# Gather and scatter of the middle slot's last token tile: from 64 rows to all 128

## The chip, the cores and the metric

The kernel runs on one core of a Trainium2 chip. The metric is device time in microseconds (us) of one execution. A profile of one execution of the kernel before, taken on the chip, stands behind every reading. In its lines PE is TensorE (PEld its weight loads), DVE is VectorE, ACT is ScalarE, POOL is GpSimd and SP is SyncE, whose queue issues the plain DMAs; POOL issues the indirect ones. A number after L is a line of the kernel.

## The reference

Eight batches of eight heads of attention over 576 positions (head size 64), where a score below the row's maximum minus `tau` is dropped; then a mixture of eight experts over the 4608 tokens, each of which goes to the one expert with the largest gate value.

```python
scores = scale * np.matmul(q, k.transpose(0, 1, 3, 2))
thresh = np.max(scores, axis=-1, keepdims=True) - tau
scores = np.where(scores >= thresh, scores, -1000000000.0)
...
logits = x @ w_gate + modality_bias[modality_id]
e_idx = np.argmax(logits, axis=1)
...
for e in range(E):
    mask = e_idx == e
    h = np.maximum(x[mask] @ w1[e], 0.0)
    out[mask] = gate_w[mask, None] * (h @ w2[e])
```

With D = 512 columns and F = 1024 hidden units per expert, the output is a matrix of 4608 rows of 512 floats.

## The kernel before

**Attention** runs over 32 pairs of heads (four per batch). Its result `xs`, one row of 512 floats per token, lies in DRAM.

**Routing.** After each batch the tokens are put into a table `tab` in DRAM: each expert has a stretch of its own in it, and a token's entry (its row number and its gate weight) is written to the next free place of its expert. An entry that no token has taken holds the row number 4608, one past the last row, and the weight 0.

**Slots.** The experts' work is cut into slots: a slot is one expert and a stretch of its table entries. Three widths exist, `SIZES = (512, 320, 256)`. Seven slots (two of 256, five of 512) run beside the attention of later batches. The last stage runs behind the attention: two slots of 512, one of 320 (the middle slot) and one of 256, always in this order. Which expert a slot serves is found on the chip: remainders of more than 320 tokens go to the slots of 512, remainders of 257 to 320 to the middle slot, and smaller ones to the slot of 256. Further slots stand behind a run-time condition, for inputs that need them.

**One slot** is the function `slot`. Its tokens are cut into tiles of 128; `TP(t)` is the number of rows of tile t. A width of 512 has four tiles, 256 has two, and the middle slot has three, of 128, 128 and 64 rows. The steps of a slot:

- `rows`: the slot's table entries are loaded as `tb`, one column per tile, always with 128 entries per tile.
- `gather(t)`: an indirect DMA, issued by POOL (L747), fetches the rows of `xs` that column t of `tb` names into `xg`, one row per partition. An index over the bound `nrow - 1` is skipped, without an error, and its partition keeps what it held.
- `xt(t)`: four transposes on PE (L761) bring `xg` into the form [column, token], and ACT and DVE split it into two parts, `xh` and `xl` (L272, L273).
- `l1`: products with `w1` on PE (L805), then the ReLU and again a split, into `hh` and `hl` (L815, L816). Where the width is no multiple of 128, POOL sets the columns of `hh` and `hl` from the width up to the next multiple of 128 to 0 (L814).
- `l2(g, t, z)`: products with `w2` on PE (L832), in two halves of the hidden units, g = 0 and 1. The tokens of tile t are the stationary side, always 128 wide, so a full 128 rows of PSUM are written. After g = 0 ACT writes PSUM times the gate weight to `y0` (L841); after g = 1 DVE adds its share into `y` (L845), and POOL issues the indirect DMA that scatters the rows of `y` to `out` (L847), again skipping indices over the bound.
- The weights come over SP's queue as `raw` and are split into a rounded part and a residual: in the last stage by ACT (L788) and, for the residual, DVE (`w1l`) or POOL (`w2l`), both at L792.

**Buffers.** In the last stage `xg` has four buffers, `y0` four, `y` two; each is used in turn, and a new use waits until the previous user's readers are through.

**Order.** During the attention PE's order is written out by hand. The order on the other engines, and on all engines in the last stage, is laid out when the program is built, by a planner that takes the instructions in the order of the code's due times, models a cost for each and tracks when buffers come free. In the last stage the code asks for the gathers of a slot well ahead of its transposes.

The change touches `gather` (L747) and the last part of `l2` (L835 to L850) and reaches only tiles with fewer than 128 rows: tile 2 of the middle slot.

Of the kernel before, what the change touches and what calls it, by code (L numbers as in the profile page):

```python
# [11 lines left out]
F32 = mybir.dt.float32  # L12
# [3 lines left out]
U32 = mybir.dt.uint32  # L16
# [8 lines left out]
def _inst(x):  # L25
    return x.ins if hasattr(x, "ins") else x
# [3 lines left out]
def tile_attn_moe(  # L30
# [20 lines left out]
    DM = H * D  # L51
    DF = w1.shape[2]
    N = B * S
    P = 128
# [8 lines left out]
    W = 512  # L63
# [23 lines left out]
    xp = ctx.enter_context(tc.tile_pool(name="xp", bufs=1))  # L87
# [103 lines left out]
    xs = dram.tile([N, DM], F32, name="xs")  # L191
# [58 lines left out]
    def tbank(hold=False):  # L250
        i = next(x for x in line if x not in held)
        line.remove(i)
        line.append(i)
        if hold:
            held.add(i)
        return banks[i]

    def let_go(t):
        for i in range(4):
            if banks[i] is t:  # L260
                held.discard(i)
                line.remove(i)
                line.append(i)
# [450 lines left out]
    def slot(where, group, nrow, WT=W, wq=lambda: wp, nbuf=(4, 3, 5), lo_eng=None, xq=None):  # L714
# [3 lines left out]
        box = {}  # L718
# [3 lines left out]
        def TP(t):  # L722

            return min(P, WT - t * P)
# [17 lines left out]
        def gather(t):  # L742
            def f():
                xg = xt_pool().tile([P, DM], F32, name="xg", bufs=nx[1])
                box[("xg", t)] = xg

                nc.gpsimd.indirect_dma_start(  # L747
                    out=xg[0:TP(t)], out_offset=None, in_=xs[0:nrow, :],
                    in_offset=bass.IndirectOffsetOnAxis(ap=box["tb"][0:TP(t), t, 0:1].bitcast(U32), axis=0),
                    bounds_check=nrow - 1, oob_is_err=False)  # L750
            return f

# [68 lines left out]
        def l2(g, t, z):  # L821
            def f():
                if z == 0:
                    box["ps"] = group()
                nt = TP(t)
                ps = box["ps"]
                ts = slice(t * P, (t + 1) * P)
                f_ = g * F2 + z
                hh, hl = box[("h", f_)]
                wh, wl = box[("w", 2, f_)]  # L830
                for y, (h, w) in enumerate(((hh, wh), (hh, wl), (hl, wh))):
                    nc.tensor.matmul(out=ps, lhsT=h[:, ts], rhs=w, start=(z == 0 and y == 0),  # L832
                                     stop=(z == F2 - 1 and y == 2))
                if z < F2 - 1:
                    return  # L835
                let_go(ps)
                ps = ps[0:nt]
                tb = box["tb"][0:nt]
                if g == 0:
                    y0 = xp.tile([P, DM], F32, name="y0", bufs=W // P)[0:nt]  # L840
                    nc.scalar.activation(out=y0, in_=ps, func=AF.Copy, scale=tb[:, t, 1:2].bitcast(F32))  # L841
                    box[("y0", t)] = y0
                    return
                y = xp.tile([P, DM], F32, name="y", bufs=2)[0:nt]
                nc.vector.scalar_tensor_tensor(out=y, in0=ps, scalar=tb[:, t, 1:2].bitcast(F32),  # L845
                                               in1=box.pop(("y0", t)), op0=ALU.mult, op1=ALU.add)
                i = _inst(nc.gpsimd.indirect_dma_start(  # L847
                    out=out, out_offset=bass.IndirectOffsetOnAxis(ap=tb[:, t, 0:1].bitcast(U32), axis=0),
                    in_=y, in_offset=None, bounds_check=N - 1, oob_is_err=False))
                for o in prev_out:  # L850
                    tc.declare_no_dep(i, o, reason="every token has a row of its own")
                prev_out.append(i)
            return f
# [111 lines left out]
    for n0, (w, nb) in zip(begins, SIDE):  # L965
# [12 lines left out]
        def when(u):  # L978

            if u < 0:  # L980
                return n0 + u * C['neg'] * W / w
            k = bisect.bisect_right(times, u) - 1
            nxt = times[k + 1] if k + 1 < len(times) else times[k] + 0.5
            x = k + min(1, (u - times[k]) / (nxt - times[k]))
            kf = math.floor(x)
            a, b = step_of(k0 + kf), step_of(k0 + kf + 1)
            return a + (x - kf) * (b - a) - 0.5
        for e in ev:

            if e[0] is None:  # L990
                t = n0 + e[2]
            elif n0 in begins[:-1]:

                which, f_ = e[3]
                t = n0 + C['w' + 'SL'[w == W]][8 * which + f_ - 8] - e[2]
            else:
                t = when(e[0]) - e[2]
# [49 lines left out]
    with tc.manual_schedule(engines={ET.PE}):  # L1047

        ps = tbank()
# [86 lines left out]
```

## Time and profile before

| | us |
|---|---|
| median of three runs | 1117.74 (1115.88 to 1118.3) |
| the profiled execution | 1116.18 |
| its span, first to last instruction | 1114.5 |

How to read what follows: the page gives each engine's busy time with its share of the span, then the span in 40 equal slices (one digit each, the busy share in tenths; for PEclk the clock granted to TensorE), the DMA queues, and shares of the chain of work that ended last, followed back from the last instruction. Timeline rows are start, duration, engine, line, operation, tile written and tiles read, and in brackets the idle time of that engine before it with what ended it. In rows of groups, "x16 | 12.0, 748 | 19.7" is the count, the busy time in us, the mean ns of one, and the idle time before them in us. Queue q0 is that of the indirect DMAs.

### The profile page before, as it was taken

What the parts mean: (1) busy time and instruction counts of PE and PEld (TensorE: products, weight loads), DVE (VectorE), ACT (ScalarE), POOL (GpSimd) and SP (SyncE); (2) the same over time, 40 slices, a digit from 0 to 9 for tenths busy, and PEclk for the clock granted to TensorE, in tenths of its full rate; (3) what the DMA queues carried; (4) which work ended last, traced back from release to release, by engine and by line L of the source; (5) the groups of instructions that cost most, each with busy time, mean ns of one, the idle gap of its engine ahead of it and who ended that gap; (6) DMA issues with size and microseconds to landing.
All of it is one profiled execution on the core that took longest, in us unless ns stands there. A gap on an engine that the chain in (4) does not pass through costs nothing.

```text
span 1114.5 us, 20778 instructions
## 1 busy us (share of the span) xinstructions
PE 1029.7 (92%) x6683; PEld 809.9 (73%) x6683; DVE 725.7 (65%) x1773; ACT 641.9 (58%) x1474; POOL 537.9 (48%) x727
## 2 busy tenths in 40 slices
PE   7799869989798989999999999999999997999993
PEld 6676647777676767787777777777767775788883
DVE  6788857787568756876676766776677645243441
ACT  5687657666565656666666666566656523434440
POOL 2232345464655563665355644565265546442440
PEclk8999989999899999999999999999999999999997
DMA  5656557656666757476635763676465214644330
GB/s 123 140 136 160 124 128 184 165 110 165 165 161 130 180 129 184 102 202 162 168 82 141 197 161 91 148 206 147 107 141 152 97 39 134 216 145 131 131 99 21
DMA packets 212646, 156.06 MB, mean 140 GB/s; under 512 B 100782, under 2 KB 172462, under 8 KB 212528
## 3 DMA queue, kind: packets, MB, share of 16 engines
q1 hardware_dynamic: 205392, 135.72, 49.1%
q0 software_dynamic: 7136, 18.92, 5.2%
q8 instruction: 55, 0.90, 0.3%
q14 instruction: 63, 0.52, 0.1%
HBM read 84.12 MB, written 19.35 MB: 93 GB/s over the span
## 4 chain that ended last, share of the span: by engine, by line
PE 57%; DVE 3%; issue 2%; DMA 2%; ACT 1%; POOL 1%; another core or an unknown queue 0%; POOLq 0%; ACTq 0%; SPq 0%
PE bk L458 8%; PE bk L832 8%; PE bk L805 8%; PE s L369 8%; PE pm L832 7%; PE pm L805 6%; PE bk L420 6%; PE bk L761 1%; PE bk L311 1%; DVE pr L404 1%; PE bk L449 1%; DVE nm L386 1%; ACT e L392 1%; DMA xg<-xs,tb 1%; PE bk L507 1%
## 5 line engine op out<-in xcount | busy, mean ns | idle before, releaser
L386 DVE TENSOR_REDUCE nm<-s 128x1 f32<-128x576 f32 x288 | 216.9, 754 | 135.1 <-PE s L369 125.2
L392 ACT ACTIVATE e<-s,nm 128x576 f32<-128x576 f32 x288 | 215.0, 747 | 113.8 <-DVE nm L386 107.2
L404 DVE SCALAR_TENSOR_TENSOR pr<-s,nm,e 128x576 f32<-128x576 f32 x288 | 231.5, 815 | 75.1 <-ACT e L392 67.4
L369 PE MATMUL s<-km,q 128*128 128x288 f32 x1024 | 202.3, 320 | 41.1 <-DMA q<-nq 17.2
L431 ACT COPY ptm<-bk 128x512 f32<-128x512 f32 x256 | 149.3, 584 | 78.4 <-PE bk L420 66.4
L369 PEld LDWEIGHTS s<-km,q 128*128 128x128 f32 x1024 | 148.5, 192 | 62.1 <-issue 33.5
L420 PE MATMUL bk<-ident,pr 128*128 128x128 f32 x1152 | 175.8, 276 | 3.9 <-ACT ptm L431 2.0
L420 PEld LDWEIGHTS bk<-ident,pr 128*128 128x128 f32 x1152 | 143.6, 142 | 27.9 <-DVE hl L816 3.0
L458 PE MATMUL bk<-ptm,v_m 128*64 128x320 f32 (+1 forms) x1024 | 144.5, 420 | 0.1
L792 POOL TENSOR_TENSOR w2l<-raw,w2h 128x512 fp32r<-128x512 f32 x88 | 113.7, 1299 | 30.9 <-ACT w2h L788 26.7
L458 PEld LDWEIGHTS bk<-ptm,v_m 128*64 128x64 f32 x1024 | 67.6, 139 | 50.1 <-issue 10.3
L790 POOL CAST w2h<-raw 128x512 fp32r<-128x512 f32 x56 | 34.2, 613 | 140.1 <-DMA raw<-in_moe_w_dram 71.1
L433 ACT COPY rp<-pr 128x64 f32<-128x64 f32 x256 | 59.3, 248 | 56.5 <-DVE pr L404 47.0
L805 PE MATMUL bk<-xh,w1h 128*128 128x512 f32 (+1 forms) x212 | 85.5, 403 | 1.1 <-ACT xh L272 0.9
L805 PE MATMUL bk<-xl,w1h 128*128 128x512 f32 (+1 forms) x212 | 77.3, 365 | 1.9 <-DVE xl L273 1.9
L805 PE MATMUL bk<-xh,w1l 128*128 128x512 f32 (+1 forms) x212 | 76.9, 363 | 0.0
L747 POOL DMA_INDIRECT xg<-xs,tb x37 | 38.2, 1034 | 79.3 <-DMA tb<-tab 55.6
L832 PE MATMUL bk<-w2h,hh 128*128 128x512 f32 x176 | 75.7, 430 | 0.0
L847 POOL DMA_INDIRECT out_dram<-y,tb x37 | 38.6, 1042 | 74.4 <-DVE y L845 53.2
L792 POOL TENSOR_TENSOR w1l<-raw,w1h 128x512 fp32r<-128x512 f32 x56 | 71.8, 1285 | 2.9
L832 PE MATMUL bk<-w2h,hl 128*128 128x512 f32 x176 | 69.4, 394 | 0.0
L792 DVE TENSOR_TENSOR w1l<-raw,w1h 128x512 fp32r<-128x512 f32 x32 | 29.0, 908 | 61.5 <-ACT w1h L788 52.0
(205 smaller groups left out, 2006.7 us busy)
## 6 DMA issues: line engine op xcount, KB each, us to landing
raw<-in_moe_w_dram SPq DMA_DIRECT2D x176, 256.0 KB
q<-nq SPq DMA_DIRECT2D x124, 256.0 KB
km<-nk SPq DMA_DIRECT2D x124, 144.0 KB
v_m<-in_v_dram SPq DMA_DIRECT2D x32, 256.0 KB
xs<-xr SPq DMA_DIRECT2D x32, 256.0 KB
k_m<-in_k_dram SPq DMA_DIRECT2D x62, 128.0 KB
q_m<-in_q_dram SPq DMA_DIRECT2D x62, 128.0 KB
vr<-in_v_dram SPq DMA_DIRECT2D x64, 16.0 KB
```

The lines of the kernel that those rows point to most:

```text
L369: nc.tensor.matmul(out=sps[:, hf, 0:SH], lhsT=a, rhs=x, start=(z == 0), stop=(z == len(passes) - 1))
L386: in_line(nc.vector.tensor_reduce(out=nm[:, 0:1], in_=sv, axis=AX.XY, op=ALU.max, negate=True), two)
L392: nc.scalar.activation(out=e, in_=sv, func=AF.Exp, bias=nm[:, 0:1])
L404: in_line(nc.vector.scalar_tensor_tensor(out=pr.rearrange("p (a x) -> p a x", a=2), in0=s2[n % 2][:, :, 0:SH], scalar=nm[:, 1:2], in1=e, o ...
L420: nc.tensor.transpose(out=ps[:, kc * P:(kc + 1) * P], in_=pr[:, kc * P:(kc + 1) * P], identity=ident)
L431: nc.scalar.copy(out=ptm[:, s, :, (c % 2) * P:(c % 2 + 1) * P], in_=pv)
L433: nc.scalar.copy(out=rp[:, i, :], in_=pr[:, SA:S])
L458: nc.tensor.matmul(out=o, lhsT=lhsT, rhs=rhs, start=start, stop=stop, skip_group_check=True)
L792: eng.tensor_tensor(out=lo, in0=raw, in1=hi.bitcast(F32), op=ALU.subtract)
L805: nc.tensor.matmul(out=ps[:, 0:WT], lhsT=a[:, cs], rhs=x[:, c, :], start=(c == 0 and z == 0), stop=(c == KC - 1 and z == 2))
L832: nc.tensor.matmul(out=ps, lhsT=h[:, ts], rhs=w, start=(z == 0 and y == 0), stop=(z == F2 - 1 and y == 2))
L847: i = _inst(nc.gpsimd.indirect_dma_start(out=out, out_offset=bass.IndirectOffsetOnAxis(ap=tb[:, t, 0:1].bitcast(U32), axis=0), in_=y, in_o ...
```

## The change

The gather of a tile fills all 128 partitions of `xg` with all 128 entries of `tb`'s column, where it took the first `TP(t)`; `y0`, `y` and the weights `tb` are no longer cut to `TP(t)` rows, so that ACT, DVE and the scatter work on 128 partitions. Table entries past the slot's width hold the row number 4608, which lies over both bounds. The transposes of `xt` still read `TP(t)` rows.

```diff
                 nc.gpsimd.indirect_dma_start(
-                    out=xg[0:TP(t)], out_offset=None, in_=xs[0:nrow, :],
-                    in_offset=bass.IndirectOffsetOnAxis(ap=box["tb"][0:TP(t), t, 0:1].bitcast(U32), axis=0),
+                    out=xg, out_offset=None, in_=xs[0:nrow, :],
+                    in_offset=bass.IndirectOffsetOnAxis(ap=box["tb"][:, t, 0:1].bitcast(U32), axis=0),
                     bounds_check=nrow - 1, oob_is_err=False)
...
-                nt = TP(t)
                 ps = box["ps"]
...
                 let_go(ps)
-                ps = ps[0:nt]
-                tb = box["tb"][0:nt]
+                tb = box["tb"]
                 if g == 0:
-                    y0 = xp.tile([P, DM], F32, name="y0", bufs=W // P)[0:nt]
+                    y0 = xp.tile([P, DM], F32, name="y0", bufs=W // P)
                     nc.scalar.activation(out=y0, in_=ps, func=AF.Copy, scale=tb[:, t, 1:2].bitcast(F32))
...
-                y = xp.tile([P, DM], F32, name="y", bufs=2)[0:nt]
+                y = xp.tile([P, DM], F32, name="y", bufs=2)
                 nc.vector.scalar_tensor_tensor(out=y, in0=ps, scalar=tb[:, t, 1:2].bitcast(F32),
                                                in1=box.pop(("y0", t)), op0=ALU.mult, op1=ALU.add)
```

## The prediction

> **What bounds the kernel now.** I read the page first: its span, the busy row, the tenths of PE and of its clock, the chain that ended last.
>
> ```profile
> span 1114.5 us, 20778 instructions
> PE 1029.7 (92%) x6683; PEld 809.9 (73%) x6683; DVE 725.7 (65%) x1773; ACT 641.9 (58%) x1474; POOL 537.9 (48%) x727
> PE   7799869989798989999999999999999997999993
> PEclk8999989999899999999999999999999999999997
> q0 software_dynamic: 7136, 18.92, 5.2%
> PE 57%; DVE 3%; issue 2%; DMA 2%; ACT 1%; POOL 1%; another core or an unknown queue 0%; POOLq 0%; ACTq 0%; SPq 0%
> ```
>
> TensorE is busy 92% of the span and carries 57% of the chain; POOL, which issues the two DMAs that change, is busy 48% and carries 1%. But these are averages, and the change touches a single place: one of 37 gathers and one of 37 scatters. So I went to that place. The order of the 13 gathers in POOL's timeline of the last stage (four for each 512-row slot, three for the middle slot, two for the last) makes the eleventh the gather that changes; of the scatters it is the third from the end. These are the rows around both, with the first gather of the stage for comparison; columns are start, duration, what ran, and the idle time before it with what ended it.
>
> ```profile
> 932.27 1.06 POOL L747 DMA_INDIRECT xg<-xs,tb  x1 [5.53 <-DMA tb<-tab]
> ...
> 993.00 1.01 POOL L747 DMA_INDIRECT xg<-xs,tb  x1 [0.31 <-issue]
> 994.34 0.96 POOL L747 DMA_INDIRECT xg<-xs,tb  x1 [0.33 <-PE bk L761]
> 995.61 1.04 POOL L847 DMA_INDIRECT out_dram<-y,tb  x1 [0.30 <-DVE xl L273]
> 996.67 3.80 POOL L792 TENSOR_TENSOR w2l<-raw,w2h 128x512 fp32r<-128x512 f32 x3
> ...
> 1003.16 1.03 POOL L847 DMA_INDIRECT out_dram<-y,tb  x1 [0.17 <-issue]
> 1017.93 5.04 POOL L792 TENSOR_TENSOR w2l<-raw,w2h 128x512 fp32r<-128x512 f32 x4 [13.73 <-ACT w2h L788]
> 1034.00 1.01 POOL L847 DMA_INDIRECT out_dram<-y,tb  x1 [11.04 <-DVE y L845]
> 1036.80 0.99 POOL L847 DMA_INDIRECT out_dram<-y,tb  x1 [1.79 <-DVE y L845]
> 1038.09 1.05 POOL L747 DMA_INDIRECT xg<-xs,tb  x1 [0.30 <-issue]
> ...
> 1074.58 5.55 POOL L792 TENSOR_TENSOR w2l<-raw,w2h 128x512 fp32r<-128x512 f32 x4 [0.19 <-ACT w2h L788]
> 1080.29 1.19 POOL L847 DMA_INDIRECT out_dram<-y,tb  x1 [0.16 <-issue]
> 1095.32 1.00 POOL L847 DMA_INDIRECT out_dram<-y,tb  x1 [13.83 <-DVE y L845]
> ```
>
> So the gather runs at 994.34 and the scatter at 1080.29. What limits that stretch is in the busy time by windows: before the gather, and from it to the last product.
>
> ```profile
> core 0: us, PE busy (x) PEld busy (x) DVE busy (x) ACT busy (x) POOL busy (x), PEclk, DMA share, GB/s
> 900.00:994.34 94.34, 86.12 (x392) 66.43 (x391) 41.61 (x98) 32.06 (x57) 47.59 (x46) 0.98 0.45 136
> 994.34:1097.09 102.75, 102.71 (x536) 87.32 (x534) 40.40 (x60) 42.98 (x79) 41.40 (x49) 1.00 0.36 114
> ```
>
> From 994.34 to 1097.09 PE is busy 102.71 of 102.75 us at full clock: 0.04 us idle in all, with DVE, ACT and POOL below half. The change removes no matmul, so there is nothing to win there but those 0.04 us, and a loss needs something that stalls PE. Pieces of the chain in order of time (start, duration, work), and PE's two rows that matter below (both are transposes of a gathered tile, L761), complete the picture.
>
> ```profile
> 1030.14 6.30 PE pm L832 x27
> ...
> 1091.46 5.61 PE pm L832 x24
> 1097.09 0.76 DVE y L845
> 1097.88 0.50 POOLq L1029
> 1098.39 0.71 POOL out_dram L847
> ```
>
> ```profile
> 939.25 0.63 PE L761 MATMUL bk<-ident,xg 128*128 128x128 f32 x4 [2.55 <-DMA xg<-xs,tb]
> ...
> 1039.81 0.46 PE L761 MATMUL bk<-ident,xg 64*128 64x64 f32 x4
> ```
>
> After the last product come the y of the last slot's second tile and its scatter. The profiled execution took 1116.18 us, 1.68 more than its span and 1.56 under the median of the three runs (1117.74); a change of the span is added to either.
>
> **The change part by part.** By instructions nothing is added or removed: one gather, one scatter, one ACT and one DVE operation each go from 64 to 128 partitions. The transposes stay at 64 rows, and the last product always filled 128 rows of PSUM.
>
> Which rows are real? Routing the reference's inputs (default seed) by hand gives 1820, 2289 and 499 tokens to three experts; after the side slots 284, 753 and 499 are left. The middle slot takes the 284: its third tile has 28 real rows. Of its 64 rows 36 are skipped by index already; the change adds 64 rows, and these are empty with any inputs, since this slot is only given to remainders of at most 320.
>
> Does a skipped row cost anything? Queue q0 moved 18.92 MB (the middle number of its row); gathers and scatters of 4608 rows of 2 KB are 2 x 4608 x 2048 = 18.87 MB, and the table's 4608 rows of 8 bytes are 0.04. The 64 rows that before already skips in each direction (13 and 15 in the last tiles of the slots with 499 and 241 tokens, 36 here) would be another 0.26: they are not moved. On POOL the gather with 36 skipped of 64 took 0.96 us and the one with 15 of 128 (1038.09) took 1.05.
>
> ```profile
> L747 POOL DMA_INDIRECT xg<-xs,tb x37: 958/1032/1263, 144.2 to 1038.1; - x37
> L747 POOL DMA_INDIRECT xg<-xs,tb x34: 996/1031/1263, 144.2 to 993.0; - x34
> L847 POOL DMA_INDIRECT out_dram<-y,tb x37: 982/1027/1298, 268.8 to 1098.1; - x37
> L841 ACT ACTIVATE y<-pm,tb 128x512 f32<-128x512 f32 x12 | 8.3, 688 | 16.7 <-PE pm L832 16.7
> L841 ACT ACTIVATE y<-pm,tb 64x512 f32<-64x512 f32 x1 | 0.7, 685 | 0.1
> L845 DVE SCALAR_TENSOR_TENSOR y<-pm,tb,y 128x512 f32<-128x512 f32 x16 | 12.0, 748 | 19.7 <-PE pm L832 16.0 <-issue 3.6
> L845 DVE SCALAR_TENSOR_TENSOR y<-pm,tb,y 64x512 f32<-64x512 f32 x1 | 0.7, 743 | 0.0
> ```
>
> These are minimum, median and maximum ns of each kind of issue (the second row: the gathers before ours alone), then the groups of L841 and L845 by shape.
>
> *Gather on POOL.* It is the shortest of its 37 (958 ns). A 128-row list costs 996 to 1263, so +0.04 to +0.30 us; I take the median, +0.07. Below nothing is excluded, as no list of 128 is shorter. Queued behind it are a scatter, four residuals of w2 and a gather, then POOL idles 13.73 us. Those residuals are for the products that start at 1030.14, 27 us after POOL is through with them at 1003.16. Cover for the +0.07: 13.7 us.
>
> *Gather's landing.* The trace has no landing time for it. Upper bound: the first gather of the stage, started at 932.27, let PE go at 939.25, so 6.98 us from start to use, PE's order included. Ours starts at 994.34 and is used at 1039.81: 45.47 us, a margin of 38.5. Even doubled, the landing stays hidden. Cost between 0 and 7 us late, 0 on the path.
>
> *ACT and DVE.* +3 ns (688 for 685) and +5 ns (748 for 743): partitions cost no time. Both engines are under half busy in this window and PE waits for neither. If the cover were gone, 8 ns.
>
> *Scatter.* Now 1.19 us, and 128-row ones take 0.98 to 1.30: -0.21 to +0.11, taken as +0.07 like the gather. After it POOL idles 13.83 us. Its landing matters only to the y of the last slot's second tile, at 1097.09, which reuses its buffer (two buffers in turn): 1097.09 - (1080.29 + 1.19) = 15.6 us of cover, and this y is on the final chain. That is the closest point of the change to the end.
>
> *Waits.* None is new: each buffer was handed over as a whole tile before, and its previous user was a full tile; the gather's own release at 994.34 is already PE's transpose of such a one.
>
> [...]
>
> *Sum:* 0.07 + 0.07 on POOL and 0.008 on ACT and DVE, all beside PE; on the path 0.0. Profiled execution 1116.2, median **1117.7 us**.
>
> **Rivals.**
>
> *Slower: the planner moves the gather.* Outside PE's hand-written part, the order on each queue is laid out when the program is built, with a modelled cost for each instruction; a list twice as long may weigh more. Place: PE's transposes at 1039.81. The point: POOL must start the gather before 1039.81 - 6.98 = 1032.8. Behind the residuals at 1017.93 it still would; behind the two scatters at 1034.00 and 1036.80, where the last slot's gather stands now (1038.09), it would be used at 1045.07, and PE stands 5.3 us: 1117.7 + 5.3 = **1123.0**. For: PE did stand 2.55 us for such a gather at 939.25. Against: the code asks for this gather early, and 38 us is far for a small change of weight.
>
> *Faster: a planner's shift the other way.* Between 900 and 994 PE idles 8.2 us, 2.55 of it before a gathered tile. If the new weights reordered that stretch so that this wait went, 1117.7 - 2.55 = **1115.2**. Against: everything there is issued ahead of the changed gather.
>
> *The change doesn't do what it says:* the 64 rows are fetched and written after all, 2 x 0.13 MB. At the 114 GB/s of the window that is 1.1 us each, under covers of 38 and 15 us: **1117.7** again, and seen only in q0's bytes (19.18 MB).
>
> *A skipped row costs as much as a moved one.* Then the scatter is at worst twice its 1.30 us, and a landing that fits the 7.0 us bound of the gather doubles: 1080.29 + 2.6 + 14 = 1096.9, still ahead of 1097.09: **1117.7**.
>
> **How the numbers follow.** Forecast (all covered) 0.85, rows moved or charged after all 0.04 (same time), planner slower 0.07, planner faster 0.04. What a measurement of this kernel can tell from no change is about 0.2%, 2.2 us; the three runs before spread over 1115.88 to 1118.3, 2.4 us, so a pair of medians without any difference falls outside on either side some 3 or 4 times in 100. That gives faster 0.04 + 0.04 = 0.08, slower 0.07 + 0.04 = 0.11, within 0.81. The unknown costs add nothing to the range, since their covers are larger than their upper ends; it is the runs' spread around 1117.7, widened to touch the faster rival and half of the way to the slower one: 1115.3 to 1120.2. The 1123.0 is left out.
>
> **What would show it.** Right: PE idle under 0.1 us between the gather and the last product; that gather near 1.03 us and that scatter between 0.98 and 1.30, both in the same places of POOL's order; q0 still 18.92 MB; y at 128x512 near 748 ns. Wrong: a wait of PE at L761 for xg in the middle slot; a wait of the last y for the scatter; PE's 8.2 idle us before 994 gone or grown, which would mean that the order was laid out anew.

## The result, and the profile after

| | before | after |
|---|---|---|
| median, us | 1117.24 (4 runs, 1115.88 to 1118.3) | 1108.01 (4 runs, 1106.0 to 1109.11) |
| the profiled execution, us | 1116.18 | 1106.0 |
| its span, us | 1114.5 | 1104.3 |

The ratio of the times is 0.9916, with a 95% interval of 0.9895 to 0.9937: the changed kernel is 0.84% faster. The forecast was no change, 1117.7 us, in a range from 1115.3 to 1120.2; the measured time lies 7.3 us under its lower end. One run of before among those taken beside the experiments was slow, 1444.78 us at a granted clock of 0.653 where the others have 0.970 to 0.979, and is left out of every median and ratio.

The page of the changed kernel, the lines that answer to those shown of before:

```profile
span 1104.3 us, 20778 instructions
PE 1030.8 (93%) x6683; PEld 810.8 (73%) x6683; DVE 724.6 (66%) x1773; ACT 641.5 (58%) x1474; POOL 536.7 (49%) x727
PE   7799869989799899999999999999999997999997
PEclk8999989999999999999999999999999999999999
q0 software_dynamic: 7200, 18.92, 5.2%
```

The instructions are as many as before, and each engine is busy for the same time within 1.2 us. A span that is 10.2 us shorter with equal work means that waiting went, and the row of PE says where: its last digit was 3 and is 7. The last slice of the span, some 28 us, held mostly idle time of PE before, and holds less now. Queue q0 moves the same 18.92 MB in 64 packets more.

Busy time by windows in the changed kernel: from the changed gather to the last product, and from there to the end of the span.

```profile
core 0: us, PE busy (x) PEld busy (x) DVE busy (x) ACT busy (x) POOL busy (x), PEclk, DMA share, GB/s
993.34:1096.06 102.72, 102.69 (x536) 87.33 (x534) 40.38 (x60) 42.97 (x79) 41.42 (x49) 1.00 0.37 113
1096.06:1104.30 8.24, 0.00 (x0) 0.00 (x0) 0.75 (x1) 0.00 (x0) 0.99 (x1) 0.81 0.15 54
```

The same view of before, its second window alone (the first stands in the prediction):

```profile
1097.09:1114.50 17.41, 0.00 (x0) 0.00 (x0) 0.75 (x1) 0.00 (x0) 0.98 (x1) 0.63 0.07 26
```

The stretch that the prediction worked on takes 102.72 us where it took 102.75. The one behind it takes 8.24 us where it took 17.41, with the same two instructions in it, one y on DVE and one scatter on POOL: 9.17 us, as much as the medians differ (1117.24 - 1108.01 = 9.23). The remaining 1.03 us of the spans' difference had come about before the last product. The time up to the last product wanders from execution to execution (it ends between 1095.4 and 1101.5 us in the twelve profiles of this document), so this 1 us isn't put down to the change.

What fills a stretch in which no engine computes? Not the busy rows but POOL's queue rows show it: instructions that the page doesn't count as busy. Each row has the line (a helper's), the operation, its count, the minimum, median and maximum in ns, and the first and last start in us. Before:

```profile
L1102 POOLq INC_SWDGE_SEM  x1: 2468/2468/2468, 1101.7 to 1101.7; - x1
L1132 POOLq DRAIN  x3: 40/107/9375, 1104.2 to 1114.2; - x3
```

And after:

```profile
L1100 POOLq INC_SWDGE_SEM  x1: 348/348/348, 1102.3 to 1102.3; - x1
L1130 POOLq DRAIN  x3: 40/107/718, 1102.7 to 1104.0; - x3
```

Before, a semaphore increment runs from 1101.7 to 1104.2, and then the longest of three drains, which comes first of them, from 1104.2 to 1113.6, 0.9 us before the end of the span. (The expectations below call it the last drain.) After, these two take 0.35 and 0.72 us: 2.12 + 8.66 = 10.78 us less. Something is given back ahead of them. POOL's timeline of the changed kernel:

```profile
992.00 1.01 POOL L747 DMA_INDIRECT xg<-xs,tb  x1 [0.31 <-issue]
993.34 1.00 POOL L747 DMA_INDIRECT xg<-xs,tb  x1 [0.33 <-PE bk L761]
994.64 1.03 POOL L845 DMA_INDIRECT out_dram<-y,tb  x1 [0.30 <-DVE xl L273]
...
1079.25 1.26 POOL L845 DMA_INDIRECT out_dram<-y,tb  x1 [0.15 <-issue]
1094.29 0.98 POOL L845 DMA_INDIRECT out_dram<-y,tb  x1 [13.78 <-DVE y L843]
1098.56 0.99 POOL L845 DMA_INDIRECT out_dram<-y,tb  x1 [3.29 <-issue]
```

And the last row of the same view of before:

```profile
1098.12 0.98 POOL L847 DMA_INDIRECT out_dram<-y,tb  x1 [1.80 <-DVE y L845]
```

Before, the last scatter started 0.28 us after its y (1097.09 + 0.75 = 1097.84). After, y ends at 1096.81 and the scatter starts at 1098.56, 1.75 us later, and the idle time is no longer put down to y but to "issue": POOL waited for nothing that the profile shows. The chain of the changed kernel, in order of time, says the same: its end passes no y and no product any more, but the scatter before it and POOL's own time.

```profile
1094.29 0.98 POOL out_dram L845
1095.27 3.08 issue
1098.36 0.50 POOLq L1027
1098.86 0.69 POOL out_dram L845
```

So 10.78 us were won and 1.75 - 0.28 = 1.47 lost, 9.31 in all; the windows say 9.17. Where the time went is thereby clear, and why the same instructions became shorter is not: nothing in the diff names them.

### The profile page after: what moved, and what is told of

It reads as the page before. It is cut to its first block, busy times and chain, and to the rows that moved or that the text cites. A ratio compares the mean times of both kernels' runs of the same rounds, so it can differ in the third digit from the quotient of the medians.

```text
span 1104.3 us, 20778 instructions
## 1 busy us (share of the span) xinstructions
PE 1030.8 (93%) x6683; PEld 810.8 (73%) x6683; DVE 724.6 (66%) x1773; ACT 641.5 (58%) x1474; POOL 536.7 (49%) x727
## 3 DMA queue, kind: packets, MB, share of 16 engines
q0 software_dynamic: 7200, 18.92, 5.2%
## 4 chain that ended last, share of the span: by engine, by line
PE 73%; DVE 10%; issue 6%; DMA 4%; POOL 4%; ACT 2%; SPq 0%; another core or an unknown queue 0%; POOLq 0%; DVEq 0%; ACTq 0%
PE s L369 13%; PE bk L458 12%; PE bk L805 10%; PE bk L831 9%; PE bk L420 9%; PE pm L831 6%; PE pm L805 5%; DVE pr L404 3%; DVE nm L386 2%; PE bk L311 2%; DMA xg<-xs,tb 2%; PE bk L761 1%; PE bk L449 1%; ACT e L392 1%; DMA q<-nq 1%
## 5 line engine op out<-in xcount | busy, mean ns | idle before, releaser
L845 POOL DMA_INDIRECT out_dram<-y,tb x37 | 38.3, 1035 | 72.9 <-DVE y L843 52.5
L831 PE MATMUL bk<-w2l,hh 128*128 128x512 f32 x176 | 69.5, 395 | 0.0
## 6 DMA issues: line engine op xcount, KB each, us to landing
km<-nk SPq DMA_DIRECT2D x124, 144.0 KB
```

Source lines behind the costliest of these rows:

```text
L845: i = _inst(nc.gpsimd.indirect_dma_start(out=out, out_offset=bass.IndirectOffsetOnAxis(ap=tb[:, t, 0:1].bitcast(U32), axis=0), in_=y, in_o ...
```

## The experiments

**The theory** (theory A of the expectations) is a supposition: POOL keeps a record of every indirect DMA that it has issued, in a room that is limited. When the room runs out, it clears what is finished; if it never does, the records stay until the end, and the increment and the long drain go through all of them. No row of a profile shows such records or their room: they are what the theory adds, and the runs test what follows from them. The kernel issues 114 indirect DMAs (40 into the table, 37 gathers, 37 scatters). Before, with 112 lists of 128 rows and two of 64, would just fit and never run out; after, with 114 of 128, would run out at the last scatter. The gain would be an accident of the last bytes of the room, and either half of the change alone could do nothing. With less room before should end as after does, and with more room after as before does.

What a list takes is an estimate from where the room ran out in the runs below, if the room is as large as the program asks and every list of 128 rows takes the same. With 16128 bytes it ran out at the 112th DMA (e5, by the wait ahead of it), so a list takes at least 16128 / 112 = 144.0 bytes; with 10240 at the 72nd (e6, by the drain: (4148 - 882) / 82 = 39.8, so 40 more than the 3 of e5), so it takes less than 10240 / 71 = 144.2. The 100th DMA with 14336 bytes (e9, by the wait ahead of it) agrees. Two lists of 64 rows with 112 of 128 ran out of 16256 bytes at the last DMA (e3), so one of 64 takes 51 to 136 bytes. Where the program asks for no size, after runs out at its 114th list, so the room is more than 113 lists and at most 114, between 16272 and 16442 bytes. The expectations count in places, nine to a list of 128 rows, which are the 144 bytes here; no run shows a place by itself.

**The rivals.** One of the two halves does it by itself: the gather of full lists, or y, `y0` and scatter on 128 partitions. Or any other change of code or layout would shift the end of the program as well.

The edits of the room's size all change one argument of the program; the number is in bytes:

```diff
-    nc = _bacc.Bacc("TRN2", target_bir_lowering=False, num_devices=1)
+    nc = _bacc.Bacc("TRN2", target_bir_lowering=False, num_devices=1, dynamic_dma_scratch_size=16256)
```

All runs in one table; POOL's queue rows, from which increment and drain are read, follow below. "Tail" is the time from the last product to the end of the span in the profiled execution, a ratio is to runs of before taken beside that run on the same chip (their medians were 1117.49 for e1 to e4, 1116.86 for e5, e6, e8 and after again, and 1117.16 us for e9 and e10), and a dash stands where there was one run alone. Where the room ran out is inferred from the waits and the drains.

| run | room asked for, bytes | ran out at DMA | increment, ns | drain, ns | tail, us | median, us | ratio, 95% |
|---|---|---|---|---|---|---|---|
| before | none | never | 2468 | 9375 | 17.4 | 1117.24 | |
| after | none | 114 | 348 | 718 | 8.2 | 1108.01 | 0.9916 (0.9895 to 0.9937) |
| e1 gather only | none | never | 2468 | 9375 | 17.6 | 1118.39 | 0.9996 (0.9973 to 1.002) |
| e2 scatter only | none | never | 2468 | 9375 | 17.4 | 1117.04 | 0.9994 (0.9969 to 1.0019) |
| e3 before, less room | 16256 | 114 | 348 | 718 | 8.1 | 1106.3 | 0.9897 (0.9854 to 0.994) |
| e4 after, more room | 16640 | never | 2468 | 9375 | 17.3 | 1117.7 | 0.9994 (0.9968 to 1.0019) |
| after again | none | 114 | 348 | 718 | 8.4 | 1106.17 | 0.9909 (0.9883 to 0.9936) |
| e5 after, 16128 | 16128 | 112 | 388 | 882 | 7.0 | 1104.85 | 0.9893 (0.9869 to 0.9916) |
| e8 before, one more | none | 115 of 115 | 348 | 718 | 8.3 | 1108.97 | 0.9922 (0.9897 to 0.9948) |
| e6 before, 10240 | 10240 | 72 | 1188 | 4148 | 10.9 | 1108.06 | – |
| e9 after, 14336 | 14336 | 100 | 628 | 1862 | 8.0 | 1106.42 | – |
| e10 after, 4096 | 4096 | 113, the last time | 368 | 800 | 6.9 | 1108.1 | 0.9911 (0.988 to 0.9943) |

### One half of the change at a time

The first has only the first part of the diff, the gather of all 128 entries:

```diff
-                    out=xg[0:TP(t)], out_offset=None, in_=xs[0:nrow, :],
-                    in_offset=bass.IndirectOffsetOnAxis(ap=box["tb"][0:TP(t), t, 0:1].bitcast(U32), axis=0),
+                    out=xg, out_offset=None, in_=xs[0:nrow, :],
+                    in_offset=bass.IndirectOffsetOnAxis(ap=box["tb"][:, t, 0:1].bitcast(U32), axis=0),
```

> The change's gather alone: tile 2 of the middle slot is gathered with 128 indices, its y and scatter stay at 64 rows. [...] Theory B (a list of 64 rows leaves something behind that the drain pays for): one of two is gone, so the drain is about halved, and the time is near 1112 us; or all of the gain is here, near 1108.

POOL's queue rows of this kernel:

```profile
L1102 POOLq INC_SWDGE_SEM  x1: 2468/2468/2468, 1101.2 to 1101.2; - x1
L1132 POOLq DRAIN  x3: 40/107/9375, 1103.7 to 1113.7; - x3
```

The second has only the rest of the diff, `y0`, `y`, the weights and the scatter on 128 partitions:

```diff
-                ps = ps[0:nt]
-                tb = box["tb"][0:nt]
+                tb = box["tb"]
```

> The change's y and scatter alone on 128 partitions; the gather stays at 64 indices. [...] Theory B: about 1112 us, or 1108 if the scatter's list was all of it.

Its queue rows:

```profile
L1100 POOLq INC_SWDGE_SEM  x1: 2468/2468/2468, 1101.8 to 1101.8; - x1
L1130 POOLq DRAIN  x3: 40/107/9375, 1104.3 to 1114.2; - x3
```

Both have before's increment and drain to the ns, and neither differs from before in time. So neither half does it by itself: the 0.84% needs both, which rules out the first rival. Halves without an effect whose sum has one speak for a threshold.

### The threshold moved to either side

Before, with the room cut to 16256 bytes (the diff above). No instruction of the kernel changes.

> [...] Theory B and theory C (the instructions lie otherwise in memory and are fetched at another time): 1117 us, as no list and no instruction differs.

POOL's queue rows of this kernel:

```profile
L1102 POOLq INC_SWDGE_SEM  x1: 348/348/348, 1102.4 to 1102.4; - x1
L1132 POOLq DRAIN  x3: 40/107/718, 1102.8 to 1104.1; - x3
```

The changed kernel, with 16640 bytes:

> The changed kernel, but with 16640 bytes per partition for the descriptors: 1040 places. Theory A: its 1026 places fit, nothing is cleared, POOL's last drain takes about 9.4 us again and the time is near 1117 us, so that the whole gain is gone. Theories B and C: 1108 us, as after the change.

Its queue rows:

```profile
L1100 POOLq INC_SWDGE_SEM  x1: 2468/2468/2468, 1102.0 to 1102.0; - x1
L1130 POOLq DRAIN  x3: 40/107/9375, 1104.5 to 1114.5; - x3
```

The two have changed places: the code of before, with less room, has the end of the changed kernel and is 1% faster; the code of the change, with more room, has the end of before and is no faster. The last scatter went along. In POOL's timeline of before with less room it has 3.28 us of idle time put down to "issue" in front of it:

```profile
1098.77 0.99 POOL L847 DMA_INDIRECT out_dram<-y,tb  x1 [3.28 <-issue]
```

and in that of the changed kernel with more room it follows its y again:

```profile
1098.48 0.98 POOL L845 DMA_INDIRECT out_dram<-y,tb  x1 [1.82 <-DVE y L843]
```

The partitions, the lists and the skipped rows have no part in the gain beyond the room that they take. The second rival falls too: no instruction and no list was changed in either of the two.

### One DMA more

If the room decides, a DMA that does nothing useful must make before faster. This one gathers 128 rows of 256 bytes early in the attention into a tile that nothing reads, one more list of 128:

```diff
+    more_ix = iota([P, 1], [[0, 1]], "more_ix", cm=1, dt=I32)
+    more_to = glob.tile([P, D], F32, name="more_to")
+
+    def one_more():
+        nc.gpsimd.indirect_dma_start(
+            out=more_to, out_offset=None, in_=q.rearrange("b h s d -> (b h s) d"),
+            in_offset=bass.IndirectOffsetOnAxis(ap=more_ix.bitcast(U32), axis=0),
+            bounds_check=N - 1, oob_is_err=False)
...
+    at(40, one_more)
```

> The kernel before with one more indirect DMA, a gather of 128 rows of 256 bytes of q into a tile that nothing reads, early in the attention. [...] Theory A: the last drain falls to 0.7 us and the kernel gets 9 to 10 us faster by doing more work, near 1108 us. If only the reserved bytes of e3 mattered, and not the count, it stays at 1117 to 1119.

POOL's queue rows of this kernel:

```profile
L1112 POOLq INC_SWDGE_SEM  x1: 348/348/348, 1107.9 to 1107.9; - x1
L1142 POOLq DRAIN  x3: 40/107/718, 1108.3 to 1109.5; - x3
```

With one useless DMA added the kernel is 0.8% faster than before (ratio 0.9922, 0.9897 to 0.9948), and its queue rows are those of the changed kernel. The room was left as it was, so the effect doesn't hang on the bytes that are set aside. The rows stand 5.5 us later than after the change, since in this profiled execution, the slowest of the four, the last product ended that much later (1101.5 for 1096.0); apart from the two instructions that were added, the order of every engine is that of before.

### Where the clearing falls

The changed kernel again, and beside it the same with 16128 bytes, where the room runs out at the 112th DMA, two before the end. That is the scatter at 1079.25 in the timeline above, behind which POOL has some 13 us to spare.

> The changed kernel itself beside the others on the same chip: 0.990 to 0.993 of the kernel before, POOL's last drain 0.7 us.

> The changed kernel with 16128 bytes per partition for the descriptors: 1008 places, so that the room runs out at the 112th of the 114 indirect DMAs (112 x 9 = 1008), the scatter of the middle slot's tile 2, behind which POOL idles 13.8 us, and no longer at the last one. Theory A: the clearing hides there, the last scatter follows its y within 0.3 us instead of 1.75, POOL's last drain finds two or three records more than in the changed kernel (about 0.9 us for 0.7), and the kernel is 1 to 1.5 us faster than the changed one, near 1106.5. If the late start of the last scatter comes from something else (an instruction fetch), it stays, and the time is that of the changed kernel.

The queue rows with 16128 bytes:

```profile
L1100 POOLq INC_SWDGE_SEM  x1: 388/388/388, 1101.0 to 1101.0; - x1
L1130 POOLq DRAIN  x3: 40/107/882, 1101.4 to 1102.9; - x3
```

And POOL's timeline of the same kernel:

```profile
1081.20 0.99 POOL L845 DMA_INDIRECT out_dram<-y,tb  x1 [1.97 <-DVE hl L816]
1094.42 0.98 POOL L845 DMA_INDIRECT out_dram<-y,tb  x1 [12.22 <-DVE y L843]
1097.22 0.98 POOL L845 DMA_INDIRECT out_dram<-y,tb  x1 [1.82 <-DVE y L843]
```

The wait has moved two rows up: 1.97 us ahead of the scatter at 1081.20, where after had 0.15, and the last scatter follows its y as it did before. What the clearing costs, 1.8 us there (the scatter's own row is 0.27 us shorter than in after), is taken from idle time, and the tail is 6.97 us instead of 8.24. The releaser named at 1081.20, `hl`, shows how such a row misleads: a clearing has no name in the profile. The lowest median of all is this one, 1104.85, but the runs of the two (1103.67 to 1106.9, and 1102.97 to 1110.8 for the changed kernel beside it) overlap, so that the 1.3 us between them are shown by the trace and not by the times.

### How the price goes with the records

Before with 10240 bytes, where the room runs out at the 72nd DMA:

> The kernel before with 10240 bytes per partition for the descriptors: 640 places, which run out at the 72nd of 114 indirect DMAs, so that 43 records are left at the end. Theory A, if a clearing takes away all finished records: the last drain is 43/114 of the way up from 0.7 to 9.4 us, about 3.7 to 4 us, and the increment before it between 0.35 and 2.47 us. If a clearing takes only as many as the next DMA needs, the drain stays near 9 us, against the 0.7 of e3.

POOL's queue rows of this kernel:

```profile
L1102 POOLq INC_SWDGE_SEM  x1: 1188/1188/1188, 1100.1 to 1100.1; - x1
L1132 POOLq DRAIN  x3: 40/107/4148, 1101.3 to 1106.1; - x3
```

The drain of 4148 ns lies above the 3.7 to 4 us expected, and the reason is in the sizes, which can now be read. Of the DMAs issued since the room last ran out, the one at which it did included, there are 1 in after, 3 with 16128 bytes and 43 with 10240, and 114 where it never did. The increments lie on one line, 20 ns each, and so do the drains, 81.67 ns each: (4148 - 882) / 40 = 81.65, (882 - 718) / 2 = 82. From 43 to 114 both rise by less than that, as if by 64 records: (9375 - 4148) / 81.67 = 64.0 and (2468 - 1188) / 20 = 64. So a clearing leaves 7 older records, and n is 8, 10, 50 and 114: drain = 65 + 81.67 n, increment = 188 + 20 n. The 7 is worked out from this fit; no row shows the records. Two more rooms, for the changed kernel, tested it: 14336 bytes (out at the 100th, n = 15 + 7 = 22) and 4096 (by the 144 bytes and the 7 out five times, from the 29th on, last at the 113th, n = 2 + 7 = 9).

> The changed kernel with 14336 bytes per partition for the descriptors: 896 places, which run out at the 100th indirect DMA. The four drains so far (9375, 4148, 882 and 718 ns) and the four increments before them (2468, 1188, 388 and 348) all lie on 65 + 81.67 n and 188 + 20 n, if n is the number of DMAs since the clearing, the one that ran out among them, plus 7 older records that a clearing leaves, and 114 where none took place. Here n = 15 + 7 = 22: a drain of 1.86 us and an increment of 0.63. If the drain is set otherwise, by the room left or by time, it needn't lie on that line.

POOL's queue rows with 14336 bytes:

```profile
L1100 POOLq INC_SWDGE_SEM  x1: 628/628/628, 1101.3 to 1101.3; - x1
L1130 POOLq DRAIN  x3: 40/107/1862, 1102.0 to 1104.4; - x3
```

> The changed kernel with 4096 bytes per partition: 256 places, which run out at the 29th indirect DMA and, if a clearing leaves 7 records beside the one that ran out, at every 21st after it: 50, 71, 92 and 113. So n = 8 + 1 = 9 at the end: a drain of 0.80 us and an increment of 0.37, and five clearings of 21 records in place of one of 106. If a clearing's cost goes with the records it clears, each takes some 0.3 us where one took about 1.5, hardly any of it on the path, and the time is that of e5_ring_112, about 1.3 us under the changed kernel. If a clearing has a fixed cost near 1.5 us, the one at the 92nd, a gather of the last stage, and the one at the 113th may show, and the time is at or over the changed kernel's.

And with 4096:

```profile
L1100 POOLq INC_SWDGE_SEM  x1: 368/368/368, 1106.3 to 1106.3; - x1
L1130 POOLq DRAIN  x3: 40/107/800, 1106.7 to 1108.1; - x3
```

The fit gives both to the ns: 188 + 20 x 22 = 628 and 65 + 81.67 x 22 = 1862; 368 and 800 for n = 9. As a time, the second is a miss: its tail is the shortest of all, 6.9 us, yet its median is 1108.1, no better than after. POOL's timeline has, for the 28th and the 29th DMA, both into the table, with 4096 bytes

```profile
465.93 1.00 POOL L617 DMA_INDIRECT tab<-pay,posi  x1 [2.44 <-DVE pk_r L632]
467.23 0.98 POOL L617 DMA_INDIRECT tab<-pay,posi  x1 [0.30 <-issue]
```

and in the changed kernel

```profile
460.11 1.00 POOL L617 DMA_INDIRECT tab<-pay,posi  x1 [2.44 <-DVE pk_r L632]
461.42 0.97 POOL L617 DMA_INDIRECT tab<-pay,posi  x1 [0.30 <-issue]
```

so this profiled execution was 5.8 us behind before the 29th DMA, at which the room first runs out by that estimate. (That DMA into the table, the 28th of before's, starts between 458.7 and 464.2 us in the other eleven profiles.) Four clearings later, at the 112th DMA, it is 5.4 us behind (1084.70 for 1079.25), so in this trace no delay has built up over them. Nor did the first of them cost anything that can be seen: the 29th DMA has 0.30 us of idle time ahead of it in both kernels. The one at the 113th DMA is to be seen, ahead of the last scatter but one:

```profile
1100.21 0.98 POOL L845 DMA_INDIRECT out_dram<-y,tb  x1 [14.25 <-DVE y L843]
```

It starts 0.76 us after its y has ended, where after has 0.28, so this clearing of some 21 records cost 0.48 us. Why the median is no lower than after's stays open; the slower stretch of this execution lies ahead of all clearings, and of the other five runs there is no trace.

The clearing with 14336 bytes is to be seen in the timeline of that kernel, ahead of the gather that had 0.31 us of idle time before it in after (at 992.00 there):

```profile
993.47 1.02 POOL L747 DMA_INDIRECT xg<-xs,tb  x1 [1.14 <-PE pm L831]
```

It cost 0.8 us of POOL's time, while PE was busy.

## Why the prediction was wrong, point by point

**The step that failed is where the sum ends.** The prediction followed the path to the last product, and behind it named "the y of the last slot's second tile and its scatter" as what comes. After that scatter, at 1099.10, the span still had 15.4 us to run, and the chain's last row, which ends there, was quoted without a question to the 15.4. They went into the sum as a constant, part of the span of before ("a change of the span is added to either"), without a reason why they should stay. Of them 11.84 us were the increment and the drain, and these depend on the room taken by the DMAs, two of which the change widens. In place of a term of 0.0 the runs showed -9.2 us behind the last product: -2.12 and -8.66 for the two, +1.47 for the clearing ahead of the last scatter (-9.31 together, 0.14 us beyond what the windows say).

**"By instructions nothing is added or removed"** held, and was the wrong thing to count. A skipped row moves no bytes, but the longer list takes more room: q0 has 64 packets more for the 128 rows that are newly skipped, in the same 18.92 MB. The question "does a skipped row cost anything?" was answered by bytes and by time at issue; the answer that mattered was room, by the estimate 144.0 to 144.2 bytes for each of the two lists where one of 64 rows takes 51 to 136.

**What held.** PE idled 102.72 - 102.69 = 0.03 us between the gather and the last product, for 0.1 forecast as the limit. The gather took 1.00 us (1.03 forecast), the scatter 1.26 (0.98 to 1.30), and the order of every engine is that of before, the widths of the lists aside, so both planner rivals fell; PE's idle time from 900 to the gather, 8.2 us in before, is 93.34 - 85.51 = 7.8. The bytes of q0 stayed, so the rows weren't moved. The groups of L839 and L843 (L841 and L845 before) now have one shape each:

```profile
L839 ACT ACTIVATE y<-pm,tb 128x512 f32<-128x512 f32 x13 | 8.9, 687 | 16.1 <-PE pm L831 15.9
L843 DVE SCALAR_TENSOR_TENSOR y<-pm,tb,y 128x512 f32<-128x512 f32 x17 | 12.7, 748 | 19.7 <-PE pm L831 19.7
```

with the forecast 748 ns for y. Behind the gather a second scatter (1003.16, in the rows shown) stands in POOL's queue, which the prediction's list of what is queued there leaves out; it changes no cover. All of it cost nothing, and e4, the whole change with the end of before, is the clean measurement of that: 0.9994 (0.9968 to 1.0019), the forecast "no change".

**Still open:** why a clearing leaves 7 records, and what sets its price. It was 1.47 us at the 114th DMA of after, 1.8 at the 112th with 16128 bytes and 0.8 at the 100th with 14336, for some 106, 104 and 92 records by the fit; with 4096 bytes it was 0.48 at the 113th and nothing to be seen at the 29th, for some 21 each. So it doesn't go by their number alone. Releasing the records in other ways than by a smaller room was not tried.

## What to carry to other kernels

Follow the span to its end: subtract the end of the last computing instruction from it, and if more than a few us are left (here 15.4 behind the last scatter), look up what the queues of the engines do there, since here busy rows and the chain left these instructions out. In a kernel with many indirect DMAs, find by runs how much room their lists take, and set the room so that it runs out shortly before the end, where POOL is idle: here 16128 bytes gave the shortest median, 1104.85 us, with the changed code (by the times not to be told from the changed kernel itself), and 16256 gave 1106.3 with the code of before, 1.1 and 1.0% under before. A gain that stands at such a threshold belongs to the threshold, not to the edit that crossed it: one DMA more (e8) or a room of 16640 bytes (e4) would have shown another verdict for the same change.

## What of the hardware was not expected

- The end of this program pays for its indirect DMAs: by the fit 81.67 ns in the long drain and 20 ns in the increment for each one since the room last ran out (and 7 before), 11.84 us for both where it never ran out, with 114 DMAs.
- A smaller room made the kernel before faster, not slower (e3, 0.9897), and with 4096 bytes, about a quarter of the 16272 to 16442 worked out above, the changed kernel is still at 0.9911 (0.988 to 0.9943).
- Running out of room cost POOL up to 1.8 us on the spot (0.8 to 1.8 where 92 records or more were cleared, 0.48 or nothing to be seen where some 21 were), and no row names it: the profile shows idle time put down to "issue", to a DVE instruction or to PE.
- A row skipped by index moves no data (q0 18.92 MB before and after) but still takes room: with 64 more skipped rows in each of the two lists the room ran out at the last scatter, and without them, or in one list alone, it never did.
